# Packed attention without zero-padded operands: eight heads' products in tiles of 64 x 32 of the array

## The chip, the core and the metric

The kernel runs on one core of a Trainium2 chip. The metric is the time of one execution on the device in microseconds; the median of three runs is compared. PE is the engine of the matrix products (TensorE), DVE, ACT and POOL are the vector, scalar and general engines, SP issues the DMAs.

## What is computed

Three parts follow each other on 8 batches of 576 tokens, 8 heads of 64 columns; everything is float32, the weights are float64 in memory.

```python
def sm_attn(qq, kk, vv):                       # softmax of qq @ kk.T / 8, times vv
    ...
p_packed = sm_attn(p, k, v)                    # 32 packed rows per batch and head
out = sm_attn(q, p_packed, p_packed)           # 576 rows per batch and head
x = out as (4608 tokens, 512)
h = x @ w_in                                   # 512 x 1024
solu = h * softmax(h); ln = layernorm(solu) * g_ln
x = ln @ w_out                                 # 1024 x 512
return max(x @ w1, x @ w2, x @ w3) @ w_out2    # 512 x 768, 768 x 512
```

## The kernel before

Phase 1 holds the packed attention and the first mixture layer (moe1). Phase 2, from some 600 us on, is the second layer (moe2): nine blocks of 512 tokens, lines 634 (three products `mp`, of which the larger is kept) and 807 (`o`). The change touches nothing in phase 2.

In phase 1 a batch goes through the steps of the class `Packed`, twice per batch where a step works on a group `g` of four heads (4 x 32 packed rows are 128 rows). Each step has a letter; the strings `st`, `f` and `f1` in CFG list the steps in the order in which they are emitted (`st` for batch 0, `f1` for batch 1, `f` for the others), and the loop over the 36 token tiles of 128 rows sets such a step wherever its own string has an F:

- K, `keys` (lines 313 to 327): p and k are turned by PE transposes (`tp`) and copied by ACT. The turned p goes to two tiles `pTz`, one with the lower 64 rows filled and one with the upper, the other half zero: `kT` has keys of even and odd number on its two row halves, and the zero rows pick one of them.
- S, `scores` (329 to 354): eight matmuls `s<-kT,pTz` of 128 rows x 32 columns, 288 keys wide, into two PSUM banks; four heads lie in the four column tiles of the array. DVE and ACT make the softmax of it; `rim` is 1/sum, masked for even and for odd heads.
- E, `weights`: the exponentials are turned, six transposes.
- V, `values` (367 to 389): 24 matmuls `pv<-vt,e1T` of 96 rows x 32 columns, 64 wide, one per head and key block. DVE writes the result twice with `rim` into `ppz`, once for even and once for odd heads, which puts zeros where the other head of the pair would stand; a transpose gives `ppT`, whose pairs of heads lie in diagonal blocks.
- M, `product` (391 to 406): `mp<-w_in_sb,ppT`, packed values times w_in, 128 rows x 64 columns (a pair of heads with the zeros of the diagonal blocks), 512 wide; `split` (250) parts each bank into Mh (ACT) and Ml (DVE).
- Q, `queries` (408 to 422): the four tiles of 128 tokens and the 64 left over are turned for a pair of heads, into `qT`.
- X, `tokens` (424 to 466): `st<-qT,ppT`, 128 rows x 64 columns, 256 or 320 tokens wide, then a softmax on DVE and ACT and a split into `ah` and `al`.

The token tiles then take `h` = `ah`, `al` times Mh, Ml (line 505), a chain on DVE and ACT, transposes `tp<-ident,u` (551) and `y`, the product with w_out (569). All of K, S, E, V, M, Q, X and line 551 share a ring of four PSUM banks, `ps_t`, handed out by `bank` (254).

The framework then sets the order of each engine's instructions, with rules and costs of its own, from the order in which they are emitted; each engine works its list in order. q, k, v and p are loaded in steps of their own (small letters), as soon as the buffer of an earlier load is free. w_in is loaded in eight pieces at the start and turned from float64 to float32 on ACT, DVE and POOL (`decode`, 112 to 141) in the first 40 us. Later DVE and POOL do the same for other weights beside the token tiles.

## Time and profile before

| | us |
|---|---|
| three runs | 1153.14, 1153.44, 1154.44 |
| median | 1153.44 |
| span of the profiled execution, first to last instruction | 1151.9 |
| PE busy in it | 1108.0 (96%) |
| DVE busy | 543.8 (47%) |
| ACT busy | 413.9 (36%) |
| POOL busy | 191.4 (17%) |

The profiled execution's span is the only time shown of it; it is 1.5 us under the median of the runs. The share of PE is a mean: its 40 slices stand at 3 to 8 tenths in the first three, at 9 in almost all others. Matmuls of PE overlap their neighbours, so the sum of their durations is larger than the time they take; the distance from one start to the next is what one costs. DVE's 47% is 60 to 90% in phase 1 and 10 to 20% in phase 2.

### The profile page before, as it was taken

The numbers are of one execution on the slowest core, as the hardware profiler recorded it, in microseconds if no ns is written. First come the engines' busy times: TensorE is split into PE (matmuls) and PEld (weight loads), VectorE is DVE, ScalarE is ACT, GpSimd is POOL, SyncE is SP. The second block draws the span as 40 slices with busy tenths as digits, with TensorE's granted clock in tenths as the row PEclk, the third lists the DMA queues.
The fourth block names the chain that finished last, engine by engine and source line by source line (L and its number), as shares of the span: only waits on it lengthen the run. The fifth ranks groups of instructions, "written<-read, shape, count | busy, mean of one in ns | idle before, by whom it ended". The sixth has DMA issues, their size and how long they took to land.

```text
span 1151.9 us, 15495 instructions
## 1 busy us (share of the span) xinstructions
PE 1108.0 (96%) x5984; PEld 855.0 (74%) x5984; DVE 543.8 (47%) x1076; ACT 413.9 (36%) x841; POOL 191.4 (17%) x187
## 2 busy tenths in 40 slices
PE   3689999999999999999989999999999999999998
PEld 2356677676767677777868888888888888888886
DVE  6898896969786776747672121111212121121110
ACT  4477565555555554435322121121212121121211
POOL 4542211111111110001241101101111011010110
PEclk8799999999999999999999999999999999999999
DMA  8743426353635340026422010010201001010101
GB/s 253 169 121 98 132 62 159 103 156 86 173 100 143 108 116 25 19 66 191 128 74 73 1 37 37 9 65 0 74 1 57 17 19 55 1 55 1 37 1 37
DMA packets 95195, 88.05 MB, mean 76 GB/s; under 512 B 47761, under 2 KB 73361, under 8 KB 95121
## 3 DMA queue, kind: packets, MB, share of 16 engines
q1 hardware_dynamic: 95120, 87.06, 26.4%
q8 instruction: 47, 0.77, 0.3%
q14 instruction: 28, 0.22, 0.1%
HBM read 63.97 MB, written 23.07 MB: 76 GB/s over the span
## 4 chain that ended last, share of the span: by engine, by line
PE 76%; DVE 6%; issue 2%; DMA 2%; ACT 1%; POOL 1%; SPq 0%; ACTq 0%; POOLq 0%; DVEq 0%
PE mp L634 36%; PE y L569 13%; PE o L807 12%; PE h L505 7%; PE tp L551 2%; PE tp L417 1%; PE mp L400 1%; DMA wdram<-dt 1%; PE s L333 1%; DMA yf<-ydram 1%; DVE ll L558 1%; DVE raw L129 1%; PE tp L324 1%; PE st L433 1%; DVE dt L126 1%
## 5 line engine op out<-in xcount | busy, mean ns | idle before, releaser
L642 DVE TENSOR_TENSOR cur<-mp,cur 128x512 f32<-128x512 f32 x108 | 74.6, 691 | 427.1 <-PE mp L634 424.3
L634 PE MATMUL mp<-yh,wh 128*128 128x512 f32 x648 | 254.6, 393 | 0.6 <-DVE cur L642 0.6
L634 PE MATMUL mp<-yl,wh 128*128 128x512 f32 x648 | 254.8, 393 | 0.0
L634 PE MATMUL mp<-yh,wl 128*128 128x512 f32 x648 | 254.3, 393 | 0.0
L647 POOL TENSOR_TENSOR hl<-cur,hh 128x512 fp32r<-128x512 f32 x54 | 70.1, 1298 | 483.3 <-ACT hh L646 483.3
L634 PEld LDWEIGHTS mp<-yh,wh 128*128 128x128 f32 x648 | 122.0, 188 | 28.8 <-DVE cur L642 1.1
L634 PEld LDWEIGHTS mp<-yl,wh 128*128 128x128 f32 x648 | 121.9, 188 | 27.9 <-DVE yl L625 0.2
L634 PEld LDWEIGHTS mp<-yh,wl 128*128 128x128 f32 x648 | 121.8, 188 | 27.7
L569 PE MATMUL y<-lh,woh 128*128 128x512 f32 x288 | 118.3, 415 | 1.5 <-ACT lh L557 1.5
L569 PE MATMUL y<-ll,woh 128*128 128x512 f32 x288 | 115.6, 401 | 0.9 <-DVE ll L558 0.9
L569 PE MATMUL y<-lh,wol 128*128 128x512 f32 x288 | 114.1, 397 | 0.0
L646 ACT CAST hh<-cur 128x512 fp32r<-128x512 f32 x54 | 33.4, 619 | 192.7 <-DVE cur L642 192.7
L640 ACT COPY cur<-mp 128x512 f32<-128x512 f32 x54 | 31.6, 586 | 160.1 <-PE mp L634 160.1
L807 PE MATMUL o<-w2h,hl 128*128 128x512 f32 x216 | 85.6, 396 | 2.1 <-POOL hl L647 2.1
L807 PE MATMUL o<-w2h,hh 128*128 128x512 f32 x216 | 85.5, 396 | 0.2 <-ACT hh L646 0.2
L807 PE MATMUL o<-w2l,hh 128*128 128x512 f32 x216 | 85.3, 395 | 0.0
L139 POOL TENSOR_TENSOR dt<-raw,dt 128x256 f32<-128x256 f32 x40 | 30.7, 768 | 214.9 <-DVE dt L134 145.7
L569 PEld LDWEIGHTS y<-lh,woh 128*128 128x128 f32 x288 | 53.9, 188 | 15.7 <-ACT lh L557 1.8
L569 PEld LDWEIGHTS y<-ll,woh 128*128 128x128 f32 x288 | 54.5, 189 | 13.1 <-DVE ll L558 2.2
L569 PEld LDWEIGHTS y<-lh,wol 128*128 128x128 f32 x288 | 54.2, 188 | 12.2
L557 ACT ACTIVATE lh<-tp,g_sb 128x512 fp32r<-128x512 f32 x72 | 47.3, 686 | 32.9 <-PE tp L551 32.6
L513 ACT ACTIVATE u<-h,nm 128x1024 f32<-128x1024 f32 x36 | 40.2, 1115 | 47.0 <-DVE nm L511 46.7
(121 smaller groups left out, 1648.3 us busy)
## 6 DMA issues: line engine op xcount, KB each, us to landing
kt<-in_k_dram SPq DMA_DIRECT2D x16, 576.0 KB, 5.6
vt<-in_v_dram SPq DMA_DIRECT2D x16, 576.0 KB, 4.8
ydram<-yt SPq DMA_DIRECT2D x36, 256.0 KB, 3.5
yf<-ydram SPq DMA_DIRECT2D x36, 256.0 KB, 3.4
out_dram<-ob SPq DMA_DIRECT2D x36, 256.0 KB, 2.1
qtl<-in_q_dram SPq DMA_DIRECT2D x64, 128.0 KB, 3.3
raw<-in_moe_w_dram SPq DMA_DIRECT2D x24, 256.0 KB, 3.0
raw<-in_moe_w_in_dram SPq DMA_DIRECT2D x8, 512.0 KB, 7.9
```

Of the source, the lines that this page charges most:

```text
L139: add.tensor_tensor(out=dst, in0=f32(hi), in1=t, op=ALU.add)
L505: nc.tensor.matmul(h[:, n, :], lhsT=x, rhs=m[:, g, n * 512:(n + 1) * 512], start=(i == 0), stop=(i == len(ops) - 1),)
L513: nc.scalar.activation(u, hv, AF.Exp, bias=nm, accum_out=sums[:, t:t + 1])
L551: nc.tensor.transpose(tp[:, i * P:(i + 1) * P], lnt[4 * j + i][:, kc * P:(kc + 1) * P], ident)
L557: nc.scalar.activation(lh, tp, AF.Copy, scale=gc)
L569: nc.tensor.matmul(ys[half][m], lhsT=w[:, kc, ms], rhs=x, start=(kc == 0 and i == 0), stop=(kc == KFF - 1 and i == 2),)
L634: nc.tensor.matmul(mp, lhsT=w[c][x][:, kc, :], rhs=yy[:, kc, :], start=(kc == 0 and i == 0), stop=(kc == KDM - 1 and i == 2),)
L640: nc.scalar.copy(nxt, mp)
L642: nc.vector.tensor_tensor(out=nxt, in0=mp, in1=cur, op=ALU.max)
L646: nc.scalar.copy(hh, cur)
L647: nc.gpsimd.tensor_tensor(out=hl, in0=cur, in1=f32(hh), op=ALU.subtract)
L807: nc.tensor.matmul(ops[i], lhsT=x[:, ts], rhs=w, start=(c == 0 and n == 0), stop=(c == KF2 - 1 and n == 2),)
```

## The change

The heads are paired differently and the zeros go.

- The query heads c and c + 4 lie on the two row halves of `qT` (before: 2c and 2c + 1), and w_in's rows are loaded so that `w_in_sb[:, c]` has the rows of heads c and c + 4; each of its eight pieces is now two DMAs.
- K copies the turned p whole (`pT`). S gives each of its eight matmuls 64 rows, the half that it needs, and takes the two halves in turn.
- V multiplies two heads' weights (64 columns) with both heads' values (128 wide): 12 matmuls per group, of which DVE keeps for each head its own part, with two masked operations, the second of which adds. The packed values of both groups stand side by side in one `ppz`, so one transpose per batch gives `ppT`, 64 rows of the array for each group.
- M and X use `by_head`: one matmul of 64 rows x 32 columns per head, eight per product, into two banks, one for each group. M's number now counts the halves of w_in's columns, not the groups.
- Q turns the four full tiles per pair of heads as before; the 64 tokens left over of two pairs are loaded as one tile of 128 rows (`qtail`) and turned once.
- The strings `st`, `f` and `f1` put M0 behind V1 and move q3.

```diff
-    st=['K0S0K1v0q0', '', 'v1', 'q1E0', 'S1V0Q0E1Q1V1M0', 'q2', 'q3Q2Q3X0X1M1', ''],
-    f=['K0q0', 'S0q1', 'K1v0E0', 'v1Q0Q1q2', 'S1V0', 'q3Q2E1', 'Q3V1', 'M0X0', 'M1X1'],
+    st=['K0S0K1v0q0', '', 'v1', 'q1E0', 'S1V0Q0E1Q1V1', 'q2q3M0', 'Q2Q3X0X1M1', ''],
+    f=['K0q0', 'S0q1', 'K1v0E0', 'v1Q0Q1q2', 'S1V0q3', 'Q2E1', 'Q3V1', 'M0X0', 'M1X1'],
...
-    f1=['q0K0', 'Q0v0q1S0', 'K1E0q2', 'Q1v1', 'V0S1', 'Q2q3E1', 'Q3V1', 'X0', 'M0X1M1'],
+    f1=['q0K0', 'Q0v0q1S0', 'K1E0q2', 'Q1v1', 'V0S1q3', 'Q2E1', 'Q3V1', 'M0', 'X0M1X1'],
...
-        raw = wide(words(w_in)[c * P:(c + 1) * P, ns, :])
+        raw = u_p.tile([P, DFF], F32, tag="u", name="raw").bitcast(I32).rearrange("r (f t) -> r f t", t=2)
+        for r in range(2):
+            nc.sync.dma_start(
+                out=raw[D * r:D * (r + 1)], in_=words(w_in)[HD * r + D * c:HD * r + D * (c + 1), ns, :]
+            )
...
-            for r in range(2):
-                ev('pTz', pTz[r][D * r:D * (r + 1), :], tp[D * r:D * (r + 1), :P])
+            self.pT = a_p.tile([P, P], F32, tag="pT", name="pT", bufs=1)
+            ev('pTz', self.pT, tp[:, :P])
...
-            for r in range(2):
-                for hh in range(4):
+            for hh in range(4):
+                for r in range(2):
+                    rows = slice(D * r, D * (r + 1))
                     nc.tensor.matmul(
                         s1[r][NP * hh:NP * (hh + 1), :HALF],
-                        lhsT=pTz[r][:, NP * hh:NP * (hh + 1)],
-                        rhs=self.kT[g][:, hh, :],
+                        lhsT=self.pT[rows, NP * hh:NP * (hh + 1)],
+                        rhs=self.kT[g][rows, hh, :],
...
-                for hh in range(4):
+                for c in range(2):
                     nc.tensor.matmul(
-                        pv[NP * hh:NP * (hh + 1), :D],
-                        lhsT=self.e1T[g][:, j, NP * hh:NP * (hh + 1)],
-                        rhs=self.vt[g][:, hh, jj * D:(jj + 1) * D],
+                        pv[64 * c:64 * (c + 1), :2 * D],
+                        lhsT=self.e1T[g][:, j, 64 * c:64 * (c + 1)],
+                        rhs=self.vt[g][:, 2 * c:2 * c + 2, jj, :],
...
+            own = self.ppz[:, g, :]
+            nc.vector.tensor_scalar_mul(own, pv[:, :D], self.rim[g][:, 0:1])
+            nc.vector.scalar_tensor_tensor(
+                out=own, in0=pv[:, D:2 * D], scalar=self.rim[g][:, 1:2], in1=own, op0=ALU.mult, op1=ALU.add
+            )
+            if g == 1:
+                ppT[b] = s_p.tile([P, P], F32, tag="ppT", name="ppT")
+                tp = bank("tp")
+                nc.tensor.transpose(tp[:, :P], self.ppz.rearrange("r a d -> r (a d)"), ident)
+                ev('ppT', ppT[b], tp[:, :P])
+
+        def by_head(self, outs, rhs):
+            for c in range(NPAIR):
+                for g in range(NG):
+                    rows = slice(D * g, D * (g + 1))
+                    nc.tensor.matmul(
+                        outs[g][NP * c:NP * (c + 1), :],
+                        lhsT=ppT[self.b][rows, NP * c:NP * (c + 1)],
+                        rhs=rhs[rows, c, :],
+                        start=True, stop=True,
+                    )
...
+            mp = [bank("mp") for _ in range(NG)]
+            self.by_head(mp, w_in_sb[:, :, ns])
+            for g in range(NG):
+                split(Mh[b][:, g, ns], Ml[b][:, g, ns], mp[g])
...
+            if c % 2:
                 tp = bank("tp")
+                nc.tensor.transpose(tp[:, :P], self.qtail[c // 2].rearrange("r h d -> r (h d)"), ident)
+                ev('qT', qT[b][:, c - 1:c + 1, full * P:], tp[:, :P].rearrange("r (i t) -> r i t", i=2), c)
...
+            st = [bank("st")[:, :n_tok] for _ in range(NG)]
+            self.by_head(st, qT[b][:, :, c0:c0 + n_tok])
             for g in range(NG):
-                nc.vector.transpose(x[:, g, :], st[:, :n_tok])
+                nc.vector.transpose(x[:, g, :], st[g])
```

Three places show how the lists of the engines move. The first is PE in batch 0, from the second group's values to the first keys of batch 1 (`pv` values, `mp` M, `qtl` and `qtail` queries, `st` tokens; the last figures are rows x columns of what is written). Before:

```order
L373 MATMUL pv<-vt,e1T 32x64 x24
L388 MATMUL tp<-ident,ppz 128x128
L400 MATMUL mp<-w_in_sb,ppT 64x512 x4
L417 MATMUL tp<-ident,qtl 128x128 x4
L417 MATMUL tp<-ident,qtl 128x64
L417 MATMUL tp<-ident,qtl 128x128 x4
L417 MATMUL tp<-ident,qtl 128x64
L433 MATMUL st<-qT,ppT 64x256 x4
L433 MATMUL st<-qT,ppT 64x320 x4
L400 MATMUL mp<-w_in_sb,ppT 64x512 x4
L316 MATMUL tp<-ident,p_sb 128x128
L324 MATMUL tp<-ident,kt 128x96 x12
```

The same place with the change:

```order
L382 MATMUL pv<-vt,e1T 64x128 x12
L398 MATMUL tp<-ident,ppz 128x128
L406 MATMUL mp<-w_in_sb,ppT 32x512 x8
L431 MATMUL tp<-ident,qtl 128x128 x8
L437 MATMUL tp<-ident,qtail 128x128
L406 MATMUL st<-qT,ppT 32x256 x8
L406 MATMUL st<-qT,ppT 32x320 x8
L406 MATMUL mp<-w_in_sb,ppT 32x512 x8
L323 MATMUL tp<-ident,p_sb 128x128
L331 MATMUL tp<-ident,kt 128x96 x12
```

Each M and each X is twice as many matmuls of half the rows and half the columns; the places of the steps are the same.

The second is PE in batch 3, where three y transposes (`tp<-ident,u`, line 551) precede M and both halves of M and X follow each other (`h` is a matmul of a token tile). Before:

```order
L551 MATMUL tp<-ident,u 128x128 x12
L400 MATMUL mp<-w_in_sb,ppT 64x512 x2
L505 MATMUL h<-Mh,ahlarge 128x512
L400 MATMUL mp<-w_in_sb,ppT 64x512 x2
L433 MATMUL st<-qT,ppT 64x320 x4
L400 MATMUL mp<-w_in_sb,ppT 64x512 x4
L433 MATMUL st<-qT,ppT 64x256 x4
L505 MATMUL h<-Ml,ahlarge 128x512
```

With the change:

```order
L561 MATMUL tp<-ident,u 128x128 x12
L406 MATMUL mp<-w_in_sb,ppT 32x512 x4
L515 MATMUL h<-Mh,ahlarge 128x512
L406 MATMUL mp<-w_in_sb,ppT 32x512 x4
L406 MATMUL st<-qT,ppT 32x320 x8
L406 MATMUL mp<-w_in_sb,ppT 32x512 x8
L406 MATMUL st<-qT,ppT 32x256 x8
L515 MATMUL h<-Ml,ahlarge 128x512
```

The sequence is kept; before, two matmuls fill one bank, now the first four already write two.

The third is SP at the start. Before:

```order
L289 DMA p_sb<-in_p_dram 128x2x64 x2
L295 DMA kt<-in_k_dram 96x4x384
L185 DMA raw<-in_moe_w_in_dram 128x1024 x2
L295 DMA kt<-in_k_dram 96x4x384
L185 DMA raw<-in_moe_w_in_dram 128x1024 x4
L299 DMA vt<-in_v_dram 96x4x384
L308 DMA qtl<-in_q_dram 128x4x64 x2
L311 DMA qtl<-in_q_dram 64x2x64
L185 DMA raw<-in_moe_w_in_dram 128x1024 x2
```

With the change:

```order
L288 DMA p_sb<-in_p_dram 128x2x64 x2
L294 DMA kt<-in_k_dram 96x4x384
L185 DMA raw<-in_moe_w_in_dram 64x1024 x4
L294 DMA kt<-in_k_dram 96x4x384
L185 DMA raw<-in_moe_w_in_dram 64x1024 x8
L298 DMA vt<-in_v_dram 96x4x384
L307 DMA qtl<-in_q_dram 128x4x64 x2
L316 DMA qtail<-in_q_dram 64x64 x4
L185 DMA raw<-in_moe_w_in_dram 64x1024 x4
```

The loads keep their order; w_in's take two issues each, and four small ones stand where one query tail did.

## Rows read from the trace of the kernel before

**Rows 1.** Stretches: length, busy us (count) of PE, PEld, DVE, ACT, POOL, clock, DMA share.

```profile
0.00:40.00 40.00, 17.01 (x180) 10.91 (x182) 28.00 (x54) 16.69 (x41) 22.91 (x29) 0.82 0.81 228
40.00:62.00 22.00, 18.73 (x93) 9.54 (x90) 17.21 (x33) 12.14 (x27) 7.19 (x6) 0.78 0.69 168
62.00:90.00 28.00, 24.96 (x224) 15.34 (x224) 26.28 (x52) 21.75 (x49) 12.10 (x9) 1.00 0.43 101
90.00:467.00 377.00, 370.60 (x2546) 270.47 (x2544) 295.60 (x664) 212.45 (x471) 58.58 (x75) 1.00 0.40 112
600.00:1152.00 552.00, 548.23 (x2374) 446.22 (x2373) 89.20 (x132) 97.45 (x165) 67.21 (x52) 1.00 0.09 30
...
37.00:44.00 7.00, 5.21 (x18) 1.89 (x18) 2.56 (x7) 1.67 (x4) 2.78 (x3) 0.59 1.04 240
```

**Rows 2.** PE's waits from 90 to 467 us: waited for, us in total, times, longest.

```profile
PE tp L324 <- ACT pTz L246: 1.3, 3, 0.6
PE tp L388 <- DVE ppz L384: 1.0, 2, 0.8
```

**Rows 3.** Groups by form: shapes, count | busy us, mean ns of one | idle before.

```profile
L333 PE MATMUL s<-kT,pTz 128*32 128x288 f32 x256 | 24.9, 444 | 1.4 <-DVE x L439 1.4
...
L384 DVE TENSOR_SCALAR ppz<-pv,rim 128x64 f32<-128x64 f32 x32 | 7.9, 274 | 2.8 <-PE pv L373 2.3 <-DVE rim L354 0.5
...
L388 PE MATMUL tp<-ident,ppz 128*128 128x128 f32 x16 | 5.0, 311 | 16.5 <-DVE ppz L384 16.5
```

**Rows 4.** PE's timeline near 243 us, scores and values: start, length in us, instruction, count.

```profile
242.88 0.40 PE L569 MATMUL y<-lh,wol 128*128 128x512 f32 x1
243.21 1.18 PE L333 MATMUL s<-kT,pTz 128*32 128x288 f32 x16
244.20 0.85 PE L373 MATMUL pv<-vt,e1T 96*32 96x64 f32 x48
244.99 0.50 PE L569 MATMUL y<-lh,woh 128*128 128x512 f32 x1
```

**Rows 5.** PE's timeline near 398 us, M and tokens.

```profile
397.45 0.39 PE L569 MATMUL y<-ll,woh 128*128 128x512 f32 x1
397.68 0.40 PE L569 MATMUL y<-lh,wol 128*128 128x512 f32 x1
398.01 1.94 PE L400 MATMUL mp<-w_in_sb,ppT 128*64 128x512 f32 x8
399.77 1.25 PE L433 MATMUL st<-qT,ppT 128*64 128x320 f32 x8
```

**Rows 6.** PE's timeline near 263 us, tokens and the first h after them.

```profile
262.93 1.06 PE L433 MATMUL st<-qT,ppT 128*64 128x256 f32 x8
263.92 0.50 PE L505 MATMUL h<-Ml,ahsmall 128*128 128x512 f32 x1
264.25 0.40 PE L505 MATMUL h<-Mh,alsmall 128*128 128x512 f32 x1
```

**Rows 7.** Timelines of the start: SP's queue, POOL, then PE.

```profile
3.70 2.43 SPq L185 DMA_DIRECT2D raw<-in_moe_w_in_dram  x4
...
38.99 1.29 POOL L139 TENSOR_TENSOR w_in_sb<-raw,dt 128x512 f32<-128x512 f32 x1
...
38.79 0.45 PE L388 MATMUL tp<-ident,ppz 128*128 128x128 f32 x1 [5.70 <-DVE ppz L384]
39.17 3.68 PE L400 MATMUL mp<-w_in_sb,ppT 128*64 128x512 f32 x8
...
44.40 2.16 PE L433 MATMUL st<-qT,ppT 128*64 128x256 f32 x16
...
57.48 0.80 PE L505 MATMUL h<-Mh,ahsmall 128*128 128x512 f32 x1
```

**Rows 8.** ACT's and DVE's timelines near 203 us, one bank of M.

```profile
202.57 0.59 ACT L251 CAST Mh<-mp 128x512 fp32r<-128x512 f32 x1
...
203.60 0.68 DVE L252 TENSOR_TENSOR Ml<-mp,Mh 128x512 fp32r<-128x512 f32 x1
```

More of the change, by code (lines that the diff above doesn't have):

```diff
@@ L92 @@
     NG = H // 4
+    HD = H * D // 2
     KFF = DFF // P
@@ L172 @@
     par = pk_p.tile([P, 2], F32, name="par")
-    pTz = [pk_p.tile([P, P], F32, name=f"pTz{r}") for r in range(2)]
     nc.gpsimd.memset(par, 0.0)
@@ L377, in values @@
                         start=(j == 0), stop=(j == KJ - 1),
                     )
-            ppz = a_p.tile([P, 2, D], F32, tag="ppz", name="ppz", bufs=1)
-            for r in range(2):
-                if CFG['pz'] == 's':
-                    nc.scalar.activation(ppz[:, r, :], pv[:, :D], AF.Copy, scale=self.rim[g][:, r:r + 1])
-                else:
-                    nc.vector.tensor_scalar_mul(ppz[:, r, :], pv[:, :D], self.rim[g][:, r:r + 1])
-            if g == 0:
-                ppT[b] = s_p.tile([P, NG, P], F32, tag="ppT", name="ppT")
@@ L387, in values @@
-            tp = bank("tp")
-            nc.tensor.transpose(tp[:, :P], ppz.rearrange("r a d -> r (a d)"), ident)
-            ev('ppT', ppT[b][:, g, :], tp[:, :P])
-        def product(self, g):
+            if g == 0:
+                self.ppz = a_p.tile([P, 2, D], F32, tag="ppz", name="ppz", bufs=1)
+            own = self.ppz[:, g, :]
[3 more added lines that the diff above has]
+            )
@@ L392, in product @@
+        def product(self, n):
             b = self.b
[L393 removed]
+            if n == 0:
                 Mh[b] = m_p.tile([P, NG, DFF], F32R, tag="Mh", name="Mh")
                 Ml[b] = m_p.tile([P, NG, DFF], F32R, tag="Ml", name="Ml")
[L396 to L406 removed]
+            ns = slice(n * 512, (n + 1) * 512)
+            mp = [bank("mp") for _ in range(NG)]
+            self.by_head(mp, w_in_sb[:, :, ns])
+            for g in range(NG):
+                split(Mh[b][:, g, ns], Ml[b][:, g, ns], mp[g])
@@ L408, in queries @@
         def queries(self, c):
             b = self.b
+            full = S // P
             if c == 0:
                 qT[b] = qt_p.tile([P, NPAIR, S], F32, tag="qT", name="qT")
-            for n, blocks in enumerate((range(3), range(3, S // P + 1))):
-                tp = bank("tp")
-                t0, t1 = blocks[0] * P, min(S, (blocks[-1] + 1) * P)
-                for j in blocks:
-                    rows = min(P, S - j * P)
-                    nc.tensor.transpose(
-                        tp[:, j * P - t0:j * P - t0 + rows],
-                        self.qt[c][:rows, j, :, :].rearrange("r h d -> r (h d)"),
-                        ident[:rows, :rows],
-                    )
-                ev('qT', qT[b][:, c, t0:t1], tp[:, :t1 - t0], n)
+            tp = bank("tp")
@@ new lines, in queries @@
+            for j in range(full):
+                nc.tensor.transpose(
+                    tp[:, j * P:(j + 1) * P], self.qt[c][:, j, :, :].rearrange("r h d -> r (h d)"), ident
+                )
+            ev('qT', qT[b][:, c, :full * P], tp, c)
+            if c % 2:
+                tp = bank("tp")
+                nc.tensor.transpose(tp[:, :P], self.qtail[c // 2].rearrange("r h d -> r (h d)"), ident)
+                ev('qT', qT[b][:, c - 1:c + 1, full * P:], tp[:, :P].rearrange("r (i t) -> r i t", i=2), c)
@@ L429, in tokens @@
             x = a_p.tile([P, NG, T2], F32, tag="e1", name="x", bufs=1)[:, :, :n_tok]
+            st = [bank("st")[:, :n_tok] for _ in range(NG)]
+            self.by_head(st, qT[b][:, :, c0:c0 + n_tok])
             for g in range(NG):
-                st = bank("st")
-                for i in range(2):
-                    nc.tensor.matmul(
-                        st[64 * i:64 * (i + 1), :n_tok],
-                        lhsT=ppT[b][:, g, 64 * i:64 * (i + 1)],
-                        rhs=qT[b][:, 2 * g + i, c0:c0 + n_tok],
-                        start=True, stop=True,
-                    )
-                nc.vector.transpose(x[:, g, :], st[:, :n_tok])
+                nc.vector.transpose(x[:, g, :], st[g])
             nb = n_tok // NP
```

39 lines of the change are left out of this document (14 added, 25 removed).

## The prediction

> **What bounds the kernel now.** I read the table of stretches first. In the 377 us from 90 to 467 us, where batches 2 to 7 pass through the packed attention beside the first mixture layer, PE is busy 370.6 us, DVE 295.6 us (78%), ACT 212.5 us; from 600 us on PE is at 99% and nothing else comes near; only the first 62 us leave PE idle for long (35.7 of 62 us busy) [rows 1]. The view of PE's waits says the same of the middle: the two largest sums there are 1.3 and 1.0 us [rows 2]. So between 90 and 467 us a microsecond of PE work that goes is a microsecond of span, unless DVE, ACT or a buffer then makes PE wait. What "PE work" costs can't be read from durations, since neighbours overlap: sixteen records of the scores' product have a mean of 444 ns (7.1 us in all) and yet follow each other through in 0.99 us [rows 3, 4]. I therefore price everything by start to next start in PE's timeline.
>
> Three things are to be seen there. Each f32 product stands as two records, two passes (128 matmuls of the program for the scores are 256 records) [rows 3]. Tiles in different columns of the array run together: the scores' 16 records of 288 columns take 0.99 us, that is 4 rounds of 4 tiles at 0.25 us, and the 8 records of 512 columns of M take 398.01 to 399.77 = 1.76 us, 4 rounds of 2 tiles at 0.44 us [rows 4, 5]. Both give 0.86 ns per column and round. And a change of the array's shape costs something on either side: from the last 128-wide matmul of y at 397.68 to the first of M it is 0.33 us where two of y are 0.23 apart; the eight st records need 0.99 us to the next instruction where 4 rounds of 256 columns are 0.88; and the first h after them holds its follower off for 0.33 us in place of 0.23 [rows 5, 6]. Together 0.10 + 0.11 + 0.10 = 0.31 us there and back, 0.15 us a change.
>
> **The change, part by part**, on PE.
> *Scores.* Eight matmuls with zero rows in four column tiles become eight with 64 rows in eight tiles. If the two row halves run together, 4 rounds become 2: -0.49 us for each of 16 groups, -7.9 us.
> *M.* Eight matmuls per batch in pairs (two runs of 1.76 us) become 16 of 64 x 32, eight at a time: 32 records in 4 rounds of 0.44 us, 1.76 us in place of 3.52: -1.76 x 8 = -14.1 us.
> *Tokens.* 4 rounds of 256 and 4 of 320 columns (0.88 + 1.10 us) become 2 and 2: -0.99 x 8 = -7.9 us.
> *Values.* This part loses. Now 48 records of 64 columns go in 12 rounds of four; they take 0.79 us with the 0.11 of the way out, 0.68 without [rows 4]. The new form has 24 records of 128 columns, two tiles at a time: still 12 rounds, each 128 x 0.86 ns = 0.11 us, 1.32 us. That is +0.64 us x 16 = +10.3 us: half of what it computes (each head's weights on the other head's values) is dropped by the two masked DVE operations behind it.
> *The transpose behind the values* is made once a batch, 8 fewer; one lasts 0.31 us and overlaps its neighbours [rows 3], so between -0.8 and -2.5 us; I take -1.
> *Query tails.* 32 transposes of 64 rows become 16 of 128 rows; the columns streamed are the same, so the gain is that the 64-row shape is gone, which the next term holds.
> *Changes of shape.* Counting along the two orders of PE, the shape changes 146 times now and 95 times after: -51 x 0.15 = -7.6 us.
> Sum on PE: -7.9 - 14.1 - 7.9 + 10.3 - 1.0 - 7.6 = **-28.2 us**, 3.5 us a batch.
>
> The term with no row behind it is that two row halves of the array work at once. Rows bound it from both sides: at worst the halves take turns, then scores, M and tokens need as many rounds as now (four column tiles together, as the scores show today [rows 4]) and 29.9 us of the sum are gone; at best they run like column tiles do. I take the full overlap, as the nearest rows, column tiles of one array, lose nothing by sharing it. The Trainium skill (TensorE: Matmul & The Clock Gate, section Measured speedup vs the span model) has nine tiles in rows and columns at 6.32 times one, sixteen at 10.6 times; no run here shows it, and by it the sum would be the full one.
>
> On the other engines: DVE keeps two operations per group for the masked values (0.27 us each today; the second is now a scalar_tensor_tensor, up to 0.4 us) [rows 3] and loses one copy of ppT a batch; ACT copies the turned p once in place of two pieces, and the queries' columns in 6 copies a batch in place of 8. On both it is one thing for another, and it lies beside PE. SP issues 8 more halves of w_in at the start and 4 more q loads a batch, some 0.6 us each as w_in's are today [rows 7]. After the start SP has room; what is queued behind them there waits for buffers.
>
> **What of it arrives.** Batch 0 is not bound by PE: the decoding of w_in runs to 40 us, and the span then hangs on the chain from the tokens' st at 44.40 us over DVE's softmax to the first h at 57.48 us [rows 7]. M before it (3.68 us, mostly at the 1.2 GHz level: 0.59 granted from 37 to 44 us, after PE had stood idle for 5.7 us [rows 1, 7]) shrinks to about 1.9, so st may start 1.5 us sooner; but six more issues stand ahead of the last loads of w_in's third chunk, 6 x 0.6 us, of which the busy DMA engines (share 0.81 to 40 us [rows 1]) hide most. I take 0, between -1.5 and +2. Of batch 1 (62 to 90 us, DVE busy 26.3 of 28 us [rows 1]) I count half. So 28.2 - 3.5 - 1.8 = 22.9 us.
>
> New waits go against that. The two halves of a product write two banks at once, and both must be free when it starts; the ring has four. In three batches of the new order M, tokens, M, tokens stand nearly back to back, and the second M needs the banks of the first: two times ACT's 0.59 us and DVE's 0.68 us [rows 8] make the second bank free some 2.0 us after M ends, and PE has only about 0.6 us of tokens until then: 1.4 us, three times. In two batches three y transposes stand right before M and hold three of the four banks; there the second bank comes one copy later, 0.7 us. That is 5.6 us; DVE, going from 78% to 83%, may add, and where h or y lies between nothing is lost. Bounds 0 and 8, I take 5.
> So -22.9 + 5 = **-18 us** on the profiled 1151.9 us: 1134. The median of the runs is 1.5 us above that span: **1135.5 us**, likely within 1127 to 1142.
>
> **Rivals.**
> *The eviction eats half* (chance 0.2). If DVE's queue is the pace in the tight places, M and tokens can't leave faster than ACT's and DVE's 0.6 to 0.7 us a bank, whatever PE does; then the 22.0 us of M and tokens are mostly waits again. For it: DVE at 94% in 62 to 90 us [rows 1]; against: 22% idle later and PE waits near nothing [rows 2]. Half of the 22.0, less what the five waits above already hold, comes back, some 8 us: 1143.5, range 1142 to 1151. The Trainium skill (TensorEngine Tiling (Array Packing), section PSUM Bottleneck) warns of just this: the copy out of PSUM may bound once tiles make the product faster.
> *The row halves take turns* (0.13). A tile's second pass, or the shared columns, keep the other half out. It decides at once: 29.9 us of gain vanish, of which batch 0 and half of batch 1 did not count: 13/16, 24.3 us. The sum is -22.9 + 24.3 = +1.4 us, all from the values' doubled rounds, the bank waits fall away too, and with 0 to 2 us more of the start it is 1155 to 1157, slower by 0.1 to 0.3%. Were the halves held for one of four passes only, half of it would be lost: -22.9 + 12.2 + 5, 1148. For it: no row shows two row halves at once; against: column tiles do it freely.
> *More than forecast* (0.07): waits stay at nothing, the start gains: 1121 to 1127.
>
> **How the numbers follow.** Forecast 0.6, the rivals 0.2, 0.13 and 0.07. A measurement of this kernel tells 0.2% (2.3 us) from no change. Faster are the forecast (0.6), the last rival (0.07), all but 0.02 of the first (0.18) and the part of the second that holds one pass of four (0.03): 0.88. Within 0.2% fall 0.02 of the first and 0.05 of the second: 0.07. Slower is the rest of the second: 0.05. The range runs from 1125, which leaves out part of the last rival, to 1148, which takes in most of the first.
>
> **What would show it.** Right: scores' 16 records from first start to next instruction in about 0.6 us, M's 16 in 0.9 to 1.0, the values' 24 in 1.4; y and h untouched; DVE above 80% between 90 us and the last tokens; the last tokens' product some 18 us sooner; from there on nothing changed. The wait of M or st for ACT and DVE new in PE's waits, about 5 us. Wrong: M's 16 records in 1.8 us (turns), or PE idle over 12 us in the middle (eviction), or the first h later than 58 us (the start).

## The result, and the profile after

The change makes the kernel slower: 1165.99 us (median of four runs, 1163.46 to 1166.93) beside 1153.29 us for the kernel before on the same chip, a ratio of 1.0105 with the interval [1.0091, 1.0119]: one per cent, and clear of the noise. 1135.5 was forecast, so the forecast fails in sign, and the time lies outside its range. The profiled execution has a span of 1164.8 us, 12.9 over that of before.

The stretches of the kernel after, with the columns of [rows 1]:

```profile
0.00:40.00 40.00, 17.57 (x127) 13.42 (x127) 26.66 (x48) 17.36 (x38) 15.18 (x25) 0.73 0.93 197
40.00:62.00 22.00, 14.55 (x114) 7.46 (x111) 15.38 (x32) 10.66 (x22) 7.84 (x6) 0.66 0.69 172
62.00:90.00 28.00, 24.00 (x181) 16.52 (x179) 22.18 (x46) 19.27 (x43) 13.91 (x10) 0.87 0.58 140
90.00:467.00 377.00, 356.55 (x2380) 266.87 (x2373) 287.06 (x648) 205.66 (x442) 58.07 (x74) 0.97 0.41 110
```

From 90 to 467 us PE is idle for 377 - 356.55 = 20.5 us, where it was 6.4 [rows 1]. At the start the DMA engines are busier (0.93 for 0.81) and move less (197 GB/s for 228), and the clock is lower in the first three stretches. The second layer is as before: from the eighth block of the table below to the end it is 669 us in both.

PE's own prices came out as forecast. PE's timeline near 130 us (scores, values) and 403 us (M, tokens), to be held beside [rows 4, 5]; a price is the distance from one start to the next row's:

```profile
129.74 0.72 PE L341 MATMUL s<-kT,pT 64*32 64x288 f32 x16
130.39 1.53 PE L382 MATMUL pv<-vt,e1T 96*64 96x128 f32 x24
131.85 0.50 PE L579 MATMUL y<-lh,woh 128*128 128x512 f32 x1
...
403.20 1.09 PE L406 MATMUL mp<-w_in_sb,ppT 64*32 64x512 f32 x16
404.09 0.64 PE L406 MATMUL st<-qT,ppT 64*32 64x256 f32 x16
404.66 0.50 PE L515 MATMUL h<-Mh,ahsmall 128*128 128x512 f32 x1
```

The scores' 16 records take 0.65 us (0.99 before), M's 16 take 0.89 (1.76 before for 8 of 128 rows), the tokens' 0.57 (0.99 [rows 6]), the values' 24 take 1.46 (0.79). So two row halves of the array do work at once, and the rival of taking turns falls.

What PE waits for from 90 to 480 us; [rows 2] holds the two largest of before, 1.3 and 1.0:

```profile
PE y L579 <- ACT woh L213: 4.5, 1, 4.5
PE y L579 <- DVE ll L568: 2.1, 1, 2.1
PE h L515 <- ACT ahlarge L475: 2.0, 1, 2.0
PE tp L398 <- DVE ppz L392: 1.8, 3, 0.9
PE st L406 <- DVE x L449: 1.4, 1, 1.4
```

Two measures locate the loss in the kernels on which the argument rests. One is the start of the first, second and eighth block of y (line 579; a block is 512 tokens). The other is PE's time between the second and the eighth block, which holds M and tokens of five batches: its own time, summed from start to next start without the idle time that the trace shows, and that idle time. Both are worked out from the PE records of the traces (us). A trace is of one execution, and not always a typical one: those of e7 and e10 took 4.7 and 6.1 us more than the medians of their runs, that of e16 2.6, so the table tells where time lies and the medians what an edit is worth:

```
kernel           block 1   block 2   block 8   span     own + idle, blocks 2 to 8
before            100.3     154.7     482.8   1151.9    324.1 +  4.0
after             111.2     169.4     495.5   1164.8    313.5 + 12.3
e1                106.4     160.8                1157.6
e3                106.9     165.5     486.3   1155.0    306.8 + 13.9
e4                 99.8     163.0     489.6   1158.9    314.1 + 12.4
e5                 93.4     160.8     486.8   1156.0    313.2 + 13.0
e6                102.4     160.1     481.6   1150.3    309.5 + 12.1
e7                105.0     163.9     480.5   1149.9    306.6 + 10.1
e9                 99.4     158.1     473.6   1141.7    303.4 + 12.2
e10               104.2     167.0     493.7   1163.0    312.4 + 14.5
e12                99.8     159.4     487.6   1157.3    309.0 + 19.0
e13               102.8     162.0     477.2   1145.2    304.7 + 10.3
e16               103.5     161.9     484.5   1154.5    308.2 + 14.4
```

After against before: 10.9 us are lost by the first block, 3.8 more by the second (y's 4.5 us for `woh` lie there), and the rest gives back only 1.8. In the middle PE has 10.6 us less to do and stands idle 8.3 longer. Of the 10.9, 3.3 are there when the first product of h starts (60.79 us, before 57.48 [rows 7]). The other 7.6 come between it and the first block: there PE stands 7.7 us (before 4.1), and the granted clock is at its 1.2 GHz level for 19 us (up to 62.7, 73.0 to 79.8, 100.3 to 110.5), before for 2.3.

### The profile page after: what moved, and what is told of

Read it like the earlier page. It is cut to its first block, busy times and chain, and to the rows that moved or that the text cites. A ratio compares the mean times of both kernels' runs of the same rounds, so it can differ in the third digit from the quotient of the medians.

```text
span 1164.8 us, 15212 instructions
## 1 busy us (share of the span) xinstructions
PE 1101.1 (95%) x5832; PEld 858.8 (74%) x5832; DVE 539.7 (46%) x1068; ACT 409.6 (35%) x809; POOL 187.1 (16%) x185
## 4 chain that ended last, share of the span: by engine, by line
PE 59%; DVE 11%; issue 8%; DMA 5%; ACT 2%; POOL 2%; SPq 0%; POOLq 0%; ACTq 0%
PE mp L644 35%; PE o L817 12%; PE y L579 6%; PE h L515 4%; DMA wdram<-dt 2%; POOL dt L140 1%; DVE raw L130 1%; PE tp L561 1%; DVE dt L127 1%; DVE ll L568 1%; DVE dt L126 1%; DVE u L525 1%; DMA wt<-wdram 1%; ACT dt L121 1%; DVE nm L521 1%
## 5 line engine op out<-in xcount | busy, mean ns | idle before, releaser
L568 DVE SCALAR_TENSOR_TENSOR ll<-tp,g_sb,lh 128x512 fp32r<-128x512 f32 x72 | 52.0, 743 | 13.0 <-ACT lh L567 12.9
```

The lines of the kernel that those rows point to most:

```text
L568: nc.vector.scalar_tensor_tensor(out=ll, in0=tp, scalar=gc, in1=f32(lh), op0=ALU.mult, op1=ALU.subtract)
```

## The experiments

Every ratio is to the kernel before, run on the same chip.

**The start: e1, e2, e5.** e1 puts one part of the change into the kernel before, the split loads:

```diff
-        raw = wide(words(w_in)[c * P:(c + 1) * P, ns, :])
+        for r in range(2):
+            nc.sync.dma_start(out=raw[D * r:D * (r + 1)], in_=words(w_in)[c * P + D * r:c * P + D * (r + 1), ns, :])
```

> The kernel before, with w_in's eight pieces each loaded by two DMAs of 64 rows (same rows to the same places). Theory 'loads': the changed kernel loses its time at the start, because the halved loads and the four small ones per query tail hold SP and the transfers in flight back; then the halves alone cost 4 to 8 us here, first h after 60 us in place of 57.5, time 1157 to 1161. Rival 'coupling': the start only shifts the first h by some 3 us which is regained, and the loss comes from waits of PE behind banks, ACT and DVE; then under 2 us, 1152 to 1155.

Measured: 1160.58 us, ratio 1.0065 [1.0046, 1.0083], within what the theory of the loads expected. The first h starts at 63.5 us; the first two blocks of y start 6.1 us later than before and everything behind stays shifted. So e1 loses nothing between the first h and the first block, and the 7.6 us that after loses there don't come from the split of w_in alone; no run isolates what they come from. The first 40 us of e1, then SP's queue at the start in before, in after and in e5 (start, length, count):

```profile
0.00:40.00 40.00, 17.10 (x177) 11.53 (x177) 23.75 (x45) 17.45 (x41) 14.14 (x26) 0.73 0.87 192
```

```profile
9.83 0.33 SPq L299 DMA_DIRECT2D vt<-in_v_dram  x1
```

```profile
5.38 9.63 SPq L185 DMA_DIRECT2D raw<-in_moe_w_in_dram  x8
15.41 0.32 SPq L298 DMA_DIRECT2D vt<-in_v_dram  x1
```

```profile
3.71 2.22 SPq L184 DMA_DIRECT2D raw<-in_moe_w_in_dram  x4
9.80 0.33 SPq L294 DMA_DIRECT2D vt<-in_v_dram  x1
```

Before, four issues of 512 KB took 2.43 us [rows 7], and vt's load was issued at 9.83; the eight halves take 9.63, and vt's load moves to 15.41 us, with those of v and q behind it. The landings in the traces show why. In all three of before, e1 and after SP issues until eight loads are under way, and then the next when one lands (in after at 8.23, 9.32 and 10.43 us, behind landings at 8.21, 9.31 and 10.42). And the halves load more slowly: w_in's pieces land 1.3 to 1.5 us apart before (512 KB each, 12.77 to 16.80 us) and 1.1 us apart in after (256 KB each, 15.32 to 21.97 us).

PE then stands 7.0 us for vt, and the granted clock falls to its 1.2 GHz level while it stands, at 21.8 us; it is back only 27 us later. Before, it falls at 22.3 us too, while PE stands 7.9 us for `ppz`, but it is back after 10 us, and low for 7 more from 35.9 on: 0.68 granted from 22 to 49 us. PE's largest wait from 0 to 62 us of after, then the stretch, which has 0.50 in e1 as well:

```profile
PE pv L382 <- DMA vt<-in_v_dram: 7.0, 1, 7.0
```

```profile
22.00:49.00 27.00, 15.59 (x121) 10.95 (x121) 21.08 (x33) 9.78 (x19) 11.97 (x9) 0.50 0.95 206
```

e2 tried to mend this in the kernel after with one DMA for both row blocks of a piece, and likewise for the query tails:

```diff
+        src = words(w_in).rearrange("(r c d) f t -> c r d f t", r=2, c=NPAIR)[c]
+        nc.sync.dma_start(out=raw, in_=src[:, :, ns, :])
```

> The changed kernel, with each piece of w_in loaded by one DMA of 128 rows and each query tail by two DMAs in place of four; all else the same. Loads: 8 to 12 us less than the changed kernel's 1166, 1154 to 1158, V's wait for vt under 2 us in place of 7.0, first h before 58.5 us. Coupling: at most 3 us less, 1163 or more.

Measured: 1223.56 us, ratio 1.0604 [1.0588, 1.062], so it is no test of the loads; this form is far slower than what it replaced. The first stretch, then SP's queue:

```profile
0.00:40.00 40.00, 7.64 (x39) 4.16 (x39) 5.65 (x13) 6.00 (x13) 5.53 (x18) 1.00 0.24 74
```

```profile
12.72 33.45 SPq L185 DMA_DIRECT2D raw<-in_moe_w_in_dram  x4
```

The DMA engines are at a share of 0.24. The Trainium skill (DMA: Bandwidth & Descriptors, section Why a DMA increments its semaphore by 16 and not by 1) says that a DMA is spread over the largest number of engines, up to 16, that divides the slowest dimension of both sides; here that dimension is 2 on the memory's side. The share and the 33 us for four issues fit it; no run varies that dimension by itself.

e5 gets whole loads in another way. A group holds the heads of one parity, so the heads on the two row halves are again neighbours in w_in and q (p is turned once for both groups besides, and the query tails take half as many loads):

```diff
-                out=raw[D * r:D * (r + 1)], in_=words(w_in)[HD * r + D * c:HD * r + D * (c + 1), ns, :]
+        nc.sync.dma_start(out=raw, in_=words(w_in)[c * P:(c + 1) * P, ns, :])
...
-            nc.sync.dma_start(out=self.kt[g], in_=k[b, hs].rearrange("h (r j) d -> r h (j d)", j=KJ))
+            nc.sync.dma_start(out=self.kt[g], in_=k[b, g::2].rearrange("h (r j) d -> r h (j d)", j=KJ))
...
-                        lhsT=self.pT[rows, NP * hh:NP * (hh + 1)],
+                        lhsT=self.pT[rows, NP * (2 * hh + g):NP * (2 * hh + g + 1)],
```

> The kernel after, but a group now holds the heads of one parity, so that a piece of w_in is again 128 rows in one DMA and a pair's query tails take one DMA per pair as before; the products, their tiles and their order stay (p is transposed once for both groups). Theory that the 64-row loads cost the start about 6.5 us (which the split w_in alone did in the kernel before): w_in's third piece lands at 17 us again, first h near 57 us, first y block near 104 us, end 1159.5 us (1157 to 1162). Rival, that the start's lateness is hidden by the work behind it in this kernel: first h earlier, end still 1164 or more. Rival, that the loads alone are the whole loss: 1153 or less.

Measured: 1157.24 us, ratio 1.0034 [1.0018, 1.0051], 8.8 us under after (0.7% by the ratios). That is at the edge of its theory's range (1157 to 1162), and it is not the whole loss. The first block of y comes 17.8 us sooner than in after, the second 8.6. Part of the 17.8 is order: 18 more products of h lie between the two blocks than in after (42 for 24). y's wait for w_out there, 4.5 us for its two parts, is no shorter than in after.

**The values and the order of the row halves: e3, e4, e6, e7, e8.** e3 takes back V alone (24 matmuls, each head by itself, one multiply), e4 turns the loops of `by_head`:

```diff
-                for c in range(2):
+                for hh in range(4):
                     nc.tensor.matmul(
-                        pv[64 * c:64 * (c + 1), :2 * D],
+                        pv[NP * hh:NP * (hh + 1), :D],
```

```diff
-            for c in range(NPAIR):
-                for g in range(NG):
+            for g in range(NG):
+                for c in range(NPAIR):
```

> The changed kernel, with the values' product per head as before (24 matmuls of 32 columns, 64 wide, four tiles at a time) and one unmasked DVE multiplication; all else the same. By the prices of PE's timeline the 24 records of 1.46 us become 48 of 0.81 us: 16 x 0.65 = 10.4 us less PE work, 1156 if PE is the bound, 1161 or more if the waits eat it.

> The changed kernel, with M's and the tokens' eight matmuls issued one group (bank) after the other in place of alternating, so that the first four need one free bank only. Coupling through the two banks: 3 to 6 us less, the waits of M and st for Ml, x and ll go. Loads: within 2 us of 1166. If the array looks ahead only over column tiles, M's 16 records take 1.8 us in place of 0.88 and it is 10 us slower.

Measured: e3 1159.07 us, ratio 1.0044 [1.0021, 1.0066]; e4 1160.89, ratio 1.0059 [1.0035, 1.0082]. e3 takes 6.7 us off PE's own time in the middle. e4 takes nothing off there (314.1 for 313.5); all it gives lies ahead of the second block. Its time is the one that was expected, but not for the reason expected: the waits of M and st for `Ml`, `x` and `ll`, which were to go, are 3.1 us from 90 to 480 us, for 3.8 in after.

e6, e7 and e8 stand on e5: with V as in e3, with V and the order, with the order alone.

> The same, and the values' product by head as in the kernel before (24 matmuls of 64 columns for a group in place of 12 of 128). Theory that the two losses stand beside each other and add up: 6.5 us for the loads and 7 us for the values, so 1152.5 us (1149 to 1156). Rival, that both act through the same waits at the start: no less than 1157 us.

> The same with both, and the scores of tokens and M written group by group, so that the first bank of a pair is complete while the second is still computed. Theory that the alternating order makes VectorE and ScalarE start late on the first bank: 1147 us (1143 to 1151), with the row halves still running together at the prices of the kernel after (M's 16 records near 0.9 us). Rival, that written so the four matmuls of a group fill the array one behind the other and the halves do not overlap: M's 16 records near 1.8 us and 1157 us or more.

> Group by group with the contiguous loads, and with the values as in the kernel after. Theory that loads (6.5 us) and order (5 us) add up: 1154.5 us (1151 to 1158). Rival, that the order only helped because the start was late: 1159 us, as with the contiguous loads alone.

Measured: e6 1152.2 us, ratio 0.9988 [0.9972, 1.0004]; e7 1146.94, 0.9954 [0.9937, 0.9972]; e8 1156.04, 1.0019 [1.0003, 1.0035]. Loads and values add up in the main (8.8 and 5.0 us, with 7.0 for the values in e3); the order is worth 1.2 us with the wide values, which the intervals don't tell from nothing, and 5.3 without, so it doesn't add. M's 16 records take 0.89 us in e7 too (below, 329.00 to 329.89), so written group by group the row halves still run together. e7 is faster than both kernels: PE does 17.5 us less in the middle than before, and still only 11.4 arrive there.

**Where the rest stays: e9 to e11.** The same place in before, after and e7, M, tokens, M, tokens of a batch, on PE:

```profile
326.34 1.94 PE L400 MATMUL mp<-w_in_sb,ppT 128*64 128x512 f32 x8
328.11 1.25 PE L433 MATMUL st<-qT,ppT 128*64 128x320 f32 x8
329.19 1.89 PE L400 MATMUL mp<-w_in_sb,ppT 128*64 128x512 f32 x8
330.90 1.03 PE L433 MATMUL st<-qT,ppT 128*64 128x256 f32 x8
331.87 0.50 PE L505 MATMUL h<-Mh,ahlarge 128*128 128x512 f32 x1
```

```profile
339.10 1.09 PE L406 MATMUL mp<-w_in_sb,ppT 64*32 64x512 f32 x16
339.98 0.74 PE L406 MATMUL st<-qT,ppT 64*32 64x320 f32 x16
340.65 0.51 PE L515 MATMUL h<-Mh,allarge 128*128 128x512 f32 x1
341.64 1.68 PE L406 MATMUL mp<-w_in_sb,ppT 64*32 64x512 f32 x16 [0.48 <-DVE Ml L249]
344.69 1.26 PE L406 MATMUL st<-qT,ppT 64*32 64x256 f32 x16 [1.36 <-DVE x L449]
345.88 0.69 PE L515 MATMUL h<-Mh,ahlarge 128*128 128x512 f32 x1
```

```profile
329.00 1.09 PE L401 MATMUL mp<-w_in_sb,ppT 64*32 64x512 f32 x16
329.89 0.74 PE L401 MATMUL st<-qT,ppT 64*32 64x320 f32 x16
331.50 1.23 PE L401 MATMUL mp<-w_in_sb,ppT 64*32 64x512 f32 x12 [0.87 <-DVE Ml L246]
...
333.52 0.50 PE L510 MATMUL h<-Mh,ahlarge 128*128 128x512 f32 x1
```

Before: 5.53 us. After: 6.78, with one product of h between, though the matmuls alone would need 2.5 us less. e7: 4.52. The first M and tokens go at their price; the second pair needs the banks of the first, and those are emptied by ACT and DVE. In after DVE and ACT do this there:

```profile
338.51 0.29 DVE L245 COPY ppT<-tp 128x128 f32<-128x128 f32 x1 [0.83 <-PE tp L398]
340.89 1.29 DVE L249 TENSOR_TENSOR Ml<-mp,Mh 128x512 fp32r<-128x512 f32 x2 [2.10 <-ACT Mh L248]
343.91 0.29 DVE L126 TENSOR_SCALAR dt<-dt 128x256 f32<-128x256 f32 x1 [1.73 <-ACT dt L121]
344.12 0.51 DVE L449 STREAM_TRANSPOSE x<-st 128x320 f32<-128x320 f32 x1
```

```profile
340.27 1.07 ACT L248 CAST Mh<-mp 128x512 fp32r<-128x512 f32 x2 [2.88 <-PE mp L406]
343.45 0.43 ACT L121 ACTIVATE dt<-raw 128x256 f32<-128x256 f32 x1 [2.10 <-issue]
343.79 1.06 ACT L248 CAST Mh<-mp 128x512 fp32r<-128x512 f32 x2
```

DVE isn't full here, it stands: the tokens' transpose has had its scores since about 340.7, but it stands in DVE's list behind a step of a weight's decoding (`dt`), which waits 1.73 us for ACT's step of the same piece, which itself stands for 2.10 us. The chain that ended last leads from that step back to the store of the piece before it, out of `dt`, of which there is one buffer:

```profile
338.07 3.28 DMA wdram<-dt
341.35 2.10 issue
343.45 0.44 ACT dt L121
```

The store lands at 343.38 us, 0.07 before the step starts; the step's own load had landed at 333.97. (From 160 to 500 us the profile puts 11 more waits of this step, 16.3 us, down to this store by name.) The store took 5.30 us from its issue, where the two stores before it took 1.87 and 1.72: a load of `kt` (576 KB) had been issued 1.0 us ahead of it and landed at 342.21. Behind the stop the granted clock is at its 1.2 GHz level, and h's products start 0.43 us apart in place of 0.23:

```profile
346.00:349.40 3.40, 3.40 (x9) 2.66 (x10) 3.40 (x8) 0.74 (x1) 0.74 (x1) 0.50 0.03 11
```

```profile
346.36 0.63 PE L515 MATMUL h<-Ml,ahlarge 128*128 128x512 f32 x1
346.79 0.63 PE L515 MATMUL h<-Mh,allarge 128*128 128x512 f32 x1
```

It is so once more from 356.3 to 359.7, behind 2.1 us in which y waits for `ll`. Before has no such stretch between 60 and 520 us.

e9 is e7 without M's low part; zeros set once stand in its place:

```diff
-                split(Mh[b][:, g, ns], Ml[b][:, g, ns], mp[g])
+                nc.scalar.copy(Mh[b][:, g, ns], mp[g])
```

> The kernel with parity loads, values per head and group order (e7), but M's low part isn't computed: zeros that are set once stand in its place, so that its product is the high part's alone. That takes four VectorE subtractions of 0.68 us a batch off the eviction of M's banks; PE's instructions are the same in number and order. Theory that the M and tokens steps, now half as long on PE, are paced by the eviction of their four banks: 1140 us (1137 to 1143), and the M and tokens stretches on PE come near 0.9 and 0.6 us. Rival, that PE loses its time elsewhere (changes of clock, h, y's wait for w_out): 1145 us or more.

e10 is e7 with the steps drawn apart, e11 has both:

```diff
-    f=['K0q0', 'S0q1', 'K1v0E0', 'v1Q0Q1q2', 'S1V0q3', 'Q2E1', 'Q3V1', 'M0X0', 'M1X1'],
+    f=['K0q0', 'S0q1', 'K1v0E0', 'v1Q0Q1q2S1', 'V0q3Q2E1', 'Q3V1', 'M0', 'X0M1', 'X1'],
```

> e7 with another order of the steps of batches 2 to 7: M's first half, tokens with M's second half, and the last tokens are three fillers with work of h and y between, in place of two (M tokens, M tokens); earlier steps are drawn together to keep nine fillers. The same work on every engine. Theory of the eviction: the second M finds its banks free, and 1143 us (1140 to 1146). Rival, that the wait only moves to the next step in VectorE's queue: 1146 us or more, with tp or y waiting for VectorE instead.

> Both, M's low part again left as zeros. Theory: with the steps apart little is left for the low part to give, so 1139 us (1136 to 1142), less below e10 than e9 is below e7. Rival, that VectorE's total work is what counts: as far below e10 as e9 is below e7.

Measured: e9 1142.55 us, ratio 0.9908 [0.9879, 0.9938]; e10 1158.73, 1.005 [1.0029, 1.007]; e11 1150.42, 0.9978 [0.996, 0.9996]. Taking 21.8 us of DVE's work away (32 banks of 0.68 [rows 8]) gives 4.4 us. The time lies within the theory's range (1137 to 1143), near its end, but the place is not the theory's: by the table e9 is 5.6 us ahead of e7 at the first block of y and takes only 1.1 us less from the second to the eighth, where 20 of the 32 banks lie, and M there stays at 1.1 us for 16 records, not 0.9. Drawing the steps apart costs 11.8 us: PE's own time grows by 5.8 in the middle and its idle time by 4.4. The waits for `Ml` stay there, and others move in. From 160 to 500 us in e10:

```profile
PE h L510 <- ACT h L527: 3.4, 3, 2.2
PE tp L556 <- DVE Ml L246: 2.7, 3, 1.4
```

And e11 lies 8.3 us below e10, where the theory wanted less than e9's 4.4 below e7 (0.7 and 0.5% by the ratios, whose intervals don't tell the two apart). So nothing here bears out the simple form of the eviction theory, that M and tokens only stand too close. e10 also draws other steps together, so it doesn't refute it by itself.

**What else could be the pace: e12 to e18.** e12 decodes w_out's second half a token tile sooner; e13 has the three strings of steps of the kernel before; e14 both; e15 `X0M0` and `X1M1` in place of `M0X0` and `M1X1`; all on e7. e16 is e13 with `amul='g'`, the last multiply of the tokens' softmax on POOL.

```diff
-        for x in CFG['s0'][t] if j < 0 else CFG['s1']:
+        for x in CFG['s0'][t] if j < 0 else CFG['s1'] if t > 6 else 'DFNTHDTTyTyyTFy':
```

> e7 with a second decoding place in each of the token tiles 4 to 6, so that the second half of w_out is decoded a tile sooner; nothing else. Theory that y's wait of 2.5 to 4.5 us for w_out near 150 us is a late decoding on VectorE behind the tokens' softmax: the wait goes, second y block 3 us sooner, 1144 us (1142 to 1146). Rival, that VectorE is the pace from 90 to 160 us whatever stands first in its queue: second y block no sooner than 162 us and 1146 to 1149 us.

> e7 with the three orders of steps of the kernel before (M's first half of batch 0 right behind its values, batch 1's first tokens ahead of M, the last queries' load a step later). Theory that the change's own order of steps costs the start of batches 0 and 1 most of the 9 us: second y block near 157 us and 1141 us (1138 to 1144). Rival, that the order is worth nothing here: within 2 us of e7, 1145 to 1149.

> e12 and e13 together. Theory that they are two different waits: 1138 us (1135 to 1142). Rival, that they are the same: the better of the two alone.

> e7 with the last two steps of batches 2 to 7 turned round inside (tokens, then M), so that VectorE begins the tokens' chain before it evicts M, and h's first operand is ready sooner. Theory that the tokens' chain of VectorE sets when h may start: 1144 us (1141 to 1147). Rival, that VectorE's total is what counts: as e7, 1145 to 1149.

> e13 with the last multiply of the tokens' softmax (x times 1/sum, 1.1 to 1.8 us, twice a batch) on GpSimd in place of VectorE. VectorE loses some 23 us of work, about what e9 took off, and the chain from the tokens' product to h's operand gets longer by what GpSimd is slower. Theory that VectorE's total work is the pace: 1142 us (1140 to 1144). Rival, that the length of the chain is the pace: 1147 us or more, with PE's h or tp waiting for GpSimd or ScalarE.

Measured: e12 1160.74 us, ratio 1.0071 [1.0052, 1.009]; e13 1146.77, 0.9946 [0.9931, 0.9961]; e14 1160.49, 1.0078 [1.0054, 1.0102], as e12 alone, the worse of the two, which neither its theory nor its rival had; e15 1146.5, 0.9944 [0.9925, 0.9962]; e16 1153.68, 0.9997 [0.9978, 1.0017]. e12 has the second block 4.5 us sooner, but the first is 5.2 sooner already, and y's wait for `woh` stays at 2.9 us, as in e7, where the theory wanted it gone. It then loses 11.9 us of span on e7 by the end: PE's idle time in the middle goes from 10.1 to 19.0 (with the second place the second layer's weights are decoded sooner too). These two orders of the steps are worth nothing that shows (e13, e15). And e16 speaks against DVE's total as the pace: DVE is busy 9.1 us less from 160 to 480 us than in e13, below, and the kernel is 6.9 us slower (0.5% by the ratios, as the two ran on different chips). It isn't refuted, since the same edit makes the tokens' chain longer.

```profile
160.00:480.00 320.00, 309.70 (x2361) 231.97 (x2360) 245.93 (x536) 173.45 (x368) 43.42 (x51) 1.00 0.41 112
```

```profile
160.00:480.00 320.00, 305.62 (x2321) 227.46 (x2321) 236.84 (x519) 168.76 (x359) 54.44 (x62) 0.99 0.41 110
```

The expectation had the multiply's cost wrong: in e13 DVE's 16 take 13.1 us, some 0.82 each, and POOL's in e16 1.17. So the chain of the tokens grew by 0.35 us a time and what the two hand-overs take; that this makes 6.9 us is not shown.

e17 (on e13) and e18 (on after) emit the first step of the decoding with the others:

```diff
-        nc.scalar.activation(t, f32(hi), AF.Abs)
+        if not late:
+            nc.scalar.activation(t, f32(hi), AF.Abs)
```

> e13 with the first step of the decoding of w_out's second half and of the second layer's weights (ScalarE, |x|) emitted with the other steps, about a token tile after the load's issue, in place of right behind it. The same work. Theory that evictions stand behind a decoding that waits for its load: PE's waits from 160 to 500 us fall from 10 us to 5 or less, 1142 us (1139 to 1144). Rival, that such a place in the list is one of many and another takes over: 1145 to 1150.

> The same edit in the kernel after alone. Theory: the stop at 341 to 346 us goes, M, tokens, M, tokens there in 4.5 us or less in place of 6.8 with one product of h between, and the time falls by 4 to 8 us, to 1158 to 1162. Rival: within 3 us of the kernel after.

Measured: e17 1149.52 us, ratio 0.9963 [0.9948, 0.9978], no faster than e13 (1146.77); e18 1164.49, 1.0081 [1.0056, 1.0106], within 3 us of after. Both are the rivals' times. In e18 the stop is still there, since the framework put the step at the same place of ACT's list:

```profile
341.99 0.43 ACT L128 ACTIVATE dt<-raw 128x256 f32<-128x256 f32 x1 [2.44 <-issue]
342.32 1.05 ACT L251 CAST Mh<-mp 128x512 fp32r<-128x512 f32 x2
```

The step waits there for the store again (issued at 337.28 us, landed at 341.91), while its own load landed at 332.16. The theory had the wrong one of the two: a later place in the list was to give the load time, and the load was not late. So the edit didn't remove what it was to remove. What a second buffer of `dt`, or a store ahead of the load of `kt`, would give was not run, and whether that place costs what it seems to cost stays open.

## Why the prediction was wrong

*The prices on PE* were right where one operation stands by itself: scores -1.0 us a batch in the middle (forecast -1.0), though the one row above has -0.34 a group for the forecast -0.49; the values +1.33 a batch (forecast +1.29); the one transpose -0.12 (forecast -0.12); queries and keys together -1.2, where -0.95 was put down to changes of shape. And the two row halves work at once, the term that had no row behind it: M's 16 records take 0.89 us. h, which was to stay untouched, takes 2.8 us more over the five batches (79.0 to 81.8).

*M and tokens* were right in price (0.89 and 0.57 us) and wrong in the sum. Forecast were -14.1 and -7.9 us, 2.75 a batch. Over five batches M and tokens go from 17.9 + 10.6 us to 11.7 + 8.7 with another 2.7 of idle time: 1.1 a batch. Three fifths of the forecast gain stay in their own steps, as waits between matmuls that are part of the start-to-start times (M's 16 records at 341.64 take 1.68 us). This is the rival "the eviction eats half" in its effect; the mechanism it named, ACT's and DVE's 0.6 to 0.7 us a bank, is not shown to be the cause: without DVE's half of the eviction (e9) the middle is 1.1 us shorter.

*"I take 0, between -1.5 and +2"*, the start, is the first step that failed. The six further issues were priced by SP's 0.6 us each and taken as hidden by DMA engines that are busy anyway; but the halves themselves load more slowly (1.1 us apart for 256 KB, where 512 KB took 1.3 to 1.5), and the loads of v, q and k stand behind them in a queue that has eight under way at most. e1 measures 6.7 us for this alone; e5, which mends it in the kernel after, gives 8.8. The prediction's own mark for it, the first h later than 58 us, was passed at 60.8. The Trainium skill (DMA: Bandwidth & Descriptors, section Rules for kernel authors) advises one transfer over 128 partitions in place of two to disjoint halves, as both halves share the same engines. That says that halves gain nothing; that they lose is what e1 shows, and the prediction weighed neither.

*"Bounds 0 and 8, I take 5"*, the new waits, is the second. PE's idle time from 90 to 467 us rose by 14.1 us (6.4 to 20.5), over the mark of 12 that was set for "wrong". Of it 4.5 are y's wait for `woh`, which no term of the prediction held. The others are spread over y, h, tp and st, each waiting for ACT or DVE; 8.3 of the 14.1 lie between the second and the eighth block.

*The clock behind a wait* was in no term either. Between the second and the eighth block it is at its 1.2 GHz level for 6.8 us, before for none. At 0.43 us for a product in place of 0.23 (the rows at 346 us above, and y in [rows 5]) that is some 3 us of PE's own time, an estimate, and of the size of h's 2.8. Ahead of the second block it is low for another 6.8 us (158.3 to 165.1), behind the 4.5 us for `woh`.

By the blocks of y, 14.7 us are lost ahead of the second, where the forecast had 1.8 to gain; from the second to the eighth 2.3 are gained, where it had 17.6 (five batches at 3.5) less most of its 5 us of waits. So a little over half of the miss lies ahead of the second block.

*The values* were priced rightly and still weighed wrongly: +10.3 us was one term of a sum of gains. Two fifths of the gains of M and tokens arrived; of this loss, 7.0 us came through in e3 and 5.0 in e6, two thirds and half.

What is settled: the loads, the values, and what the stop at 341 us waits for. What isn't: what else than the loads delays the first block in after; why e7, with 17.5 us less PE work in the middle, gets 11.4 of it, and why e10, e12 and e16, which do the same work or less, are 7 to 14 us slower than their base. In all three PE's idle time in the middle grows by 4 to 9 us and its own time by 2 to 6, at many places. Some of the own time is the clock: between the second and the eighth block it is low for 10.2 us in e10 and 6.8 in e12, for 3.4 in e7; for 3.4 in e16, for none in e13. At the price above that is some 3, 1.5 and 1.5 us. All engines work lists whose order the framework sets anew with every edit, and a step that waits holds up whatever stands behind it; that this is the cause of the rest fits the place at 341 us and was not shown by a run.

## What to carry to other kernels

Price a removed matmul only up to the point where its output bank is empty and its successor's is free: here matmuls twice as fast kept two fifths of their gain, though e9 shows that the eviction's own time is not the whole of it. Before splitting a load for the sake of a layout, look for a pairing of the data that keeps it whole; regrouping the heads by parity (e5) gave the same tiles with w_in's loads whole. Ask of a stalled step which of its waits ends last, as a store out of a single buffer looks like a late load (e18). A gain and a loss on the engine that bounds don't arrive in the same share (here two fifths, and half to two thirds): of a change with terms of both signs, try the gains without the losses first (e7, 0.9954 [0.9937, 0.9972]; with the steps of before, e13, 0.9946 [0.9931, 0.9961]).

## What the runs showed of the hardware

Sixteen records in eight tiles of 64 x 32 take 0.89 us for 512 columns, the same per column and round as four column tiles did before [rows 4, 5]: for M using two row halves at once costs nothing that shows. The scores' 0.65 us and the tokens' 0.57 are some 0.15 us over that price; the change of shape behind them is in these figures. Loads of the same bytes in DMAs of 64 rows went slower than in DMAs of 128 at a higher share of busy DMA engines (e1: 192 GB/s at 0.87 in the first 40 us, beside 228 at 0.81), with no more than eight loads of SP under way in either, and a DMA whose memory side begins with a dimension of 2 brought the start to 74 GB/s. A 128 KB store issued 1.0 us behind a 576 KB load took 5.30 us to land, in place of 1.7 to 1.9. A wait of PE can cost twice: behind 4.5 us for `woh` the granted clock was 0.50 for 6.8 us, behind the stop at 341 us for 3.4, and products of 512 columns then started 0.43 us apart in place of 0.23. Near 20 us the level fell in both kernels while PE stood, and was back after 10 us in before and 27 in after; what that costs is not shown, as PE is busy only 15.6 of these 27 us.
